# A transformer block on one core: the first token tile projected from centred rows, the last tile cut at column 336, and a new hand-written order

## Chip, cores, metric

The kernel runs on one core of one Trainium2 chip. The metric is the device time of one execution in microseconds (us); less is better. A core has TensorE (PE, with its weight loads shown as PEld), VectorE (DVE), ScalarE (ACT), GpSimd (POOL) and SyncE (SP). SP, ACT and POOL issue DMAs.

## What is computed

```
x = A_x                                   # 1 x 2048 x 448, bf16
xn = (x - mean) / sqrt(var + 1e-5)        # per row
q, k, v = xn @ wqkv                       # 16 heads of 28
attn: row s sees rows s, s-2, ..., s-14;  softmax(q.k * 28**-0.5) . v, then @ wo
g = silu(gelu(xn @ w1 + b1) @ w2 + b2)    # 448 -> 1792 -> 448
```

The kernel returns x + attn * g: lines 696 and 700 add the input row block and store it.

## The kernel before, in words

The 2048 rows are taken as two halves, even and odd positions, so that a window of every second row becomes a window of neighbours. They are cut into 16 tiles of 128 rows, and four tiles make a chunk of 512. A tile is normalised on DVE (L330, L334, L364, L369; the root is on ACT, L342, its reciprocal on DVE, L345), turned so that features lie on partitions (tiles 0 to 3 by PE, L379, with a copy out of PSUM at L229 or L231; the others by a DMA transpose, L277), and kept in xnT.

PE then does five kinds of product. Queries and keys (L455) and values (L478) have 448 columns, the first feed-forward product (L513) has 512. These three are split into pairs of 64-row halves: job a uses the upper half of the array's rows while job b uses the lower one, then they change places behind a hop over POOL or SP (L412 to L426). The second feed-forward product (L547, 14 matmuls a tile), and the output projection (L682, 4 a tile) use all 128 rows. Attention is in nine blocks; a block is 64 small matmuls of scores (L596, 32 rows by 64 columns of the array, four PSUM banks) and 64 of values (L628, 64 by 32, two banks). Between them ACT takes the exponential (L606) and POOL or DVE multiplies with a mask (L612). Behind the values a string of four DVE operations, twice a block, divides by the sum: transpose L638, reciprocal L642, transpose back L647, multiply into oT L652, which also gives the bank back. The last tile's two products are cut into two parts of 224 columns (L526 to L529). A tile ends with DVE's product of attention and gate (L688, L690), the sum with x (L696) and a DMA from SP (L700). All products share eight PSUM banks, p_b, taken in order of release.

The first two tiles take another path, first_batch (L428): the three 128-row blocks of the q, k and v weights (w_in, kt 0 to 2) are used with all 128 rows as they land, three matmuls for each of the two tiles and each block; the last 64 rows (w_in3) follow.

Each of the 942 tasks names an engine, what it needs, and the buffers that it takes and gives. Which engine it runs on and where it stands is not decided by a scheduler: the string ORDER (L17) lists every task by number with a letter for its engine (P for PE, V DVE, A ACT, G POOL, S SP, D the landing of a DMA), and emit (L95) writes the instructions in just that order. So each engine's queue is the subsequence of its letter.

At the start SP issues x of tile 0, block 0 of w_in, block 2, x of tiles 2 and 3, block 1, the two parts of w_in3, then w1. ACT issues x of tile 1. POOL makes the identity, clears b1r, loads b1 into it as rows (b1r, L308) and makes the masks (L728 to L735). PE turns b1r into a column (L769) behind the first batch. Until data is there PE multiplies zeros (L244, 17 times).

Of the kernel before, what the change touches and what calls it, by code (L numbers as in the profile page):

```python
# [10 lines left out]
ALU = mybir.AluOpType  # L11
# [6 lines left out]
D0 V1 G21 S38 A40 V19 V20 P2 V26 S42 V27 G54 D39 V28 G55 V29 V30 P3 V31 V32 S48 V33 D41 V34 G35 V22 V23 G36 P4 V24  # L18
G37 V25 D43 S44 P5 A57 S46 P6 G104 S50 P7 D49 V64 P8 S52 P9 V65 S80 G106 V68 A66 P10 D45 S82 V67 P11 P12 V110 P13
S84 P14 P15 D47 V111 P112 V69 S86 P113 G108 A70 P16 V114 P17 S90 P18 V71 A115 D116 P136 V117 D51 S92 V118 P119 D53  # L20
P120 S94 V72 P140 A121 D56 D81 A122 D123 P137 V73 V76 A74 P138 V75 V124 P139 V125 V77 D83 V105 P126 A78 A58 P127 D85
V107 P141 D87 V79 V128 D129 P142 V130 V131 P153 V109 A143 D91 V144 A148 P132 G154 P133 V149 S145 P155 A134 D135 V147
P194 A156 P312 D93 V157 G172 D95 A152 V98 G174 P317 D173 S158 D146 G313 V99 G176 V88 P314 G318 G178 V89 P319 V195
V100 G182 A315 S150 P160 G180 V101 D159 V96 A316 G103 P167 V97 A320 P322 A321 G161 G168 V204 G102 D151 P162 V205
V208 S206 V209 P169 A163 V164 G323 P324 A170 V171 S210 D207 P327 G184 A325 V200 V201 G186 V196 P332 A326 S202 D211
V197 G328 G188 P329 G333 G190 S198 P334 D203 G192 A330 P231 G250 A331 S165 D199 G284 P238 A335 G232 G256 P233 A336
G239 D183 S276 P240 D185 S278 V235 A234 D187 P219 S280 D189 D191 P212 G220 D193 S236 P221 D166 G213 P214 A222 V223
S282 P337 A215 V216 S224 D237 P342 G338 P339 G343 A241 V242 P344 A340 D277 S217 P532 A341 P537 D279 A345 G533 A346
P534 G538 D285 P539 D175 A535 V300 D177 P542 A536 D179 V301 V294 S243 D181 P547 A540 G543 D218 V295 V298 A541 P544
V299 G548 V309 P549 A545 V310 V303 P552 D244 A546 V304 V307 P557 A550 G553 V308 V305 A551 P554 D281 G558 V306 V296  # L30
G311 P559 A555 V297 P562 A556 P226 A560 V435 G563 D283 G302 V436 P564 V431 A561 S437 V432 V427 P245 A565 V428 V423
G227 S433 P228 V424 A566 A59 G246 D438 P247 V230 A229 P695 S429 A248 V249 D434 G252 P517 G286 S425 G288 D287 V359
P518 D430 G290 V360 A696 G292 A698 S361 V697 G254 D289 V347 P713 A700 D291 P512 G258 V519 D293 A702 D251 G260 V699
D362 A520 V701 G262 P513 A714 V521 A716 D253 V703 D255 A718 V715 G717 P527 D257 V514 A720 D259 V719 D261 A515 V721
D263 P572 V516 D225 V348 V351 S349 P573 V352 V355 V356 D426 S353 P522 V574 D350 A575 S357 P704 P731 V576 D354 P523
G264 A732 V705 G266 A734 V706 D265 V707 G268 A736 P528 D267 V524 D358 G270 A738 V708 G272 A525 P363 G274 D269 V529
D271 P370 V709 A530 D273 G364 G733 D275 P365 V531 S371 P372 V710 G735 A366 V367 P382 A373 V374 S368 P389 G383 V711
G737 P384 V712 S390 S375 D369 P391 V739 A385 V386 P857 A392 V393 S387 P722 P749 D376 V858 P577 G401 A750 V859 S394
V723 G405 A752 G751 A754 P578 V724 D388 V725 S860 A756 V726 G753 P567 V579 D395 V727 A580 G755 P740 P767 V728 V729
P568 G757 A768 V730 D861 A770 D402 V526 A772 D406 P867 G769 V569 A774 P458 V868 A570 P465 V869 G459 V581 S870 P460  # L40
G466 V741 G771 D871 P467 A461 V462 P453 A468 V469 S463 P472 G454 V742 G773 V743 P455 S473 S470 D464 V744 P474 G775
A456 V457 P439 A475 V476 P446 G440 D471 V745 P441 G447 V746 V747 P448 A442 V443 P872 A449 V450 S444 P862 V873 P582
V863 S451 D445 V874 V864 P758 P785 V748 S875 P583 S865 A786 V759 D452 G477 A788 G787 V760 V761 A790 P877 V762 A792
A60 G789 P377 D866 V584 D876 P587 V763 A585 S378 G791 V764 P379 V765 S588 P589 V766 A380 G793 P592 A381 V571 V878
P597 G411 S593 V879 G413 D412 P594 V586 A590 S598 G415 S880 D414 P599 G419 A591 D881 P396 D416 G403 A595 D420 G407
P602 D404 S397 A596 G409 D408 P398 A600 D410 G603 P607 A601 V399 P604 A400 G417 S608 P609 G421 D418 A605 G478 P612
D422 A606 G480 D479 P617 A610 D481 G613 G482 A611 G484 P614 D483 S618 G486 D485 P619 A615 G488 D487 P776 A616 P794
D489 G490 V777 P627 A620 G492 V778 D491 V779 A621 A61 G494 D493 P632 V780 G496 D495 V781 G498 D497 V782 P892 G500
D499 V783 G502 D501 P628 V784 G504 D503 V893 G506 D505 V894 P803 G508 D507 V629 P633 S895 A804 G510 D509 V795 A630
D896 G805 D511 V796 A806 P622 V634 A808 G807 V631 A635 P821 V797 A810 P623 G809 V798 A822 A824 V636 P637 G811 A826  # L50
V624 A828 V799 G823 A625 P812 P839 V800 V626 P638 A840 G825 V813 A842 V814 A844 P897 V815 G827 A846 A62 V639 P882
V898 A640 G829 P642 V883 P647 V899 G643 G841 V816 S900 P644 V884 S648 D901 V641 G843 P649 S885 A645 V817 P652 D886
A646 G845 V818 V819 P887 A650 S653 V820 A651 G847 P654 V888 P657 A655 V889 V801 S890 P662 A656 G658 V802 D891 P659
G663 P664 A660 P907 A661 P912 A665 V908 A666 P830 V909 P848 V913 S910 P667 V914 D911 V831 P672 S915 G668 V832 D916
V833 P669 G673 V834 P674 A670 V835 P677 A671 V836 V837 A675 P681 V838 A676 A63 V849 P678 V850 V851 V852 P917 V679
P682 V853 A680 P922 V918 P902 V683 V919 A684 P685 V903 S920 V904 D921 P686 S905 V923 D906 V924 P927 V687 S925 P689
V854 A688 D926 V855 P690 V856 P692 A691 P693 V928 V929 P932 A694 P937 S930 V933 D931 V934 S935 V938 D936 V939 S940
D941
# [61 lines left out]
def kernel(  # L120
# [19 lines left out]
    KT = 4  # L140
# [45 lines left out]
    xnT = sb("xnT", [P, KT, S])  # L186
    qkT = sb("qkT", [P, 2, G, S])
# [39 lines left out]
    def copy(e, o, i):  # L227
        if e == "ACT":
            nc.scalar.copy(o, i)  # L229
        else:  # L230
            nc.vector.tensor_copy(o, i)  # L231
# [10 lines left out]
    for i in range(17):  # L242
        def fn(k, n=512 if i < 9 else P):
            nc.tensor.matmul(buf(p_b, k)[:, :n], warm[:, :P], warm[:, :n], start=True, stop=True)  # L244
        t_warm = plan.add("PE", fn, [t_warm], take=(p_b,))
        t_warm.give = ((p_b, t_warm, 0),)
# [49 lines left out]
    def load_w(kt):  # L296
        t_w.append([dma("SP", w_in[:, kt, :], A_wqkv[kt * P:(kt + 1) * P, :])])
# [64 lines left out]
    def norm(t):  # L362
# [11 lines left out]
        halves, apart = [], t < 2  # L374
# [7 lines left out]
        n = 2 if t < 2 else 4  # L382
        copied = []
        for k0 in range(0, KT, n):
            def f4(k, k0=k0, b=halves[k0 // 2 if apart else 0]):
                copy(k.on, xnT[:, k0:k0 + n, t * P:(t + 1) * P], half_bank(buf(p_b, b))[:, k0:k0 + n, :])
            b = halves[k0 // 2 if apart else 0]
            copied.append(plan.add(("DVE", "ACT"), f4, [halves[(k0 + n - 1) // 2]], give=((p_b, b, 0),)))
        t_xT01[t], t_xT[t] = copied[0], plan.add("DMA", None, copied)
# [38 lines left out]
    def first_batch(tiles, tiles0=0):  # L428

        f = []  # L430
        for kt in range(3):
            for i, js in enumerate(tiles):
                def f1(k, kt=kt, i=i, js=js):
                    for q, j in enumerate(js):
                        j.part(buf(p_b, f[i] if kt else k, q), kt, 2, kt == 0, False)
                f.append(plan.add("PE", f1, ([t_xT01[tiles0 + i]] if kt < 2 else js[0].deps[:1]) + t_w[kt] + f[i:i + 1] * (kt > 0) + f[:1] * (i > 0), take=() if kt else (p_b,) * len(js) ))
# [12 lines left out]
    def qk_rows(t, which):  # L449
        cs = slice(t * P, (t + 1) * P)  # L450

        def part(ps, kt, half, start, stop):
            r = half_rows(half)
            w = w_in[r, kt, which * D:(which + 1) * D] if kt < 3 else w_in3[r, 0, :]
            return nc.tensor.matmul(ps[:, :D], xnT[r, kt, cs], w, start=start, stop=stop)  # L455

        def evac(a, own, i):
            b = qk_tok[t % len(qk_tok)]

            def fn(k):  # L460
                copy(k.on, b[:, which, :, :DH], buf(p_b, own, i)[:, :D].rearrange("p (h c) -> p h c", h=H))
            t_row[t].append(plan.add(("ACT", "DVE"), fn, [a, t_qz[t % len(qk_tok)], t_qk.get(t - len(qk_tok))], give=((p_b, own, i),)))
# [3 lines left out]
        return _Job(D, part, [t_xT[t]] + t_w[0] + t_w[1] + t_w[2], evac, (), t_w[3])  # L466
# [5 lines left out]
    def vproj(t):  # L472
        k0 = t * P

        def part(ps, kt, half, start, stop):
            r = half_rows(half)
            w = w_in[r, kt, 2 * D:] if kt < 3 else w_in3[r, 1, :]
            return nc.tensor.matmul(ps[:, :D], xnT[r, kt, k0:k0 + P], w, start=start, stop=stop)  # L478

        def evac(a, own, i):  # L480
            def fn(k):
                copy(k.on, v_tok[t][:, :, :DH], buf(p_b, own, i)[:, :D].rearrange("p (h c) -> p h c", h=H))
# [352 lines left out]
```

## Time and profile before

| what | value |
|---|---|
| time, median of 3 runs (lowest, highest) | 156.43 us (156.08, 156.59) |
| the profiled execution's own time | 157.63 us |
| its span, first to last instruction | 155.8 us |
| mean granted TensorE clock | 0.999 |
| busy: PE, DVE, ACT, POOL | 149.6, 110.9, 85.5, 74.2 us |
| chain that ended last: PE's share | 89% |
| first product of data at (L379), first of L513 at | 5.54, 14.17 us |
| start of the last group of products (L682) | 151.06 us |
| last output DMA issued, landed | 153.05 us, 1.5 us later |

The span is the time between first and last instruction of the profiled execution; its own time has 1.83 us beside it, and the median of the runs is 1.20 us below it. So differences are worked out in the span and then taken off the median.

### The profile page before, as it was taken

Reading aid. Unit: us, or ns where it says so; the run is one execution under the profiler, and the core shown is the slowest. Engines: PE = TensorE matmul, PEld = TensorE weight load, DVE = VectorE, ACT = ScalarE, POOL = GpSimd, SP = SyncE. Lnnn points to the kernel's source line nnn. Section 1 sums busy time; section 2 is a strip of 40 time slices with the busy share of each in tenths; the row PEclk is TensorE's granted clock in tenths of the full one; section 3 lists DMA queues with packets and bytes.
Section 4 is the critical chain, followed back from the end, with each engine's and each line's share of the span. In section 5 each row is a group of like instructions: output and inputs, shape, how many; then the busy total and the mean of one; then the engine's idle time right before and its main releaser. Section 6 shows DMA issues by size and latency. Waiting matters only on the chain.

```text
span 155.8 us, 5305 instructions
## 1 busy us (share of the span) xinstructions
PE 149.6 (96%) x2204; PEld 77.3 (50%) x2204; DVE 110.9 (71%) x254; ACT 85.5 (55%) x156; POOL 74.2 (48%) x123
## 2 busy tenths in 40 slices
PE   6899999999999999999999999999999999999990
PEld 2444444444455556554654544446556434545590
DVE  4679571387166768997799898107989996997672
ACT  3438657277888615425634196778186677192130
POOL 7852867000347808639543078389799690000000
PEclk9999999999999999999999999999999999999999
DMA  5999996999936433079219730323300010200211
GB/s 144 323 300 285 122 212 151 213 343 263 196 67 131 127 67 89 21 154 130 57 36 124 112 98 22 89 58 86 91 30 4 17 49 29 61 6 0 74 39 34
DMA packets 33575, 17.36 MB, mean 111 GB/s; under 512 B 25331, under 2 KB 32387, under 8 KB 33552
## 3 DMA queue, kind: packets, MB, share of 16 engines
q1 hardware_dynamic: 31472, 14.03, 42.8%
q0 software_dynamic: 1936, 2.88, 7.3%
q8 instruction: 17, 0.28, 0.8%
q10 hardware_dynamic: 144, 0.11, 0.3%
q14 instruction: 6, 0.05, 0.1%
HBM read 7.06 MB, written 1.84 MB: 57 GB/s over the span
## 4 chain that ended last, share of the span: by engine, by line
PE 89%; DMA 4%; DVE 2%; ACT 1%; SPq 1%; issue 0%; DVEq 0%
PE bank L547 28%; PE bank L513 27%; PE bank L455 12%; PE bank L682 8%; PE bank L478 6%; DMA x_sb<-in_A_x_dram 4%; PE bank L596 4%; PE bank L628 4%; ACT L317 1%; SPq L264 1%; DVE st L330 1%; DVE sg L688 1%; DVE xn L364 0%; ACT qk_tok L229 0%; PE bank L379 0%
## 5 line engine op out<-in xcount | busy, mean ns | idle before, releaser
L547 PE MATMUL bank<-w,h 128*128 128x448 bf16 (+1 forms) x238 | 45.2, 342 | 0.0
L513 PE MATMUL bank<-xnT,w 64*128 64x512 bf16 x392 | 44.3, 376 | 0.0
L517 ACT ACTIVATE h<-bank,b 128x512 bf16<-128x512 f32 x56 | 34.1, 687 | 15.2 <-PE bank L513 15.1
L271 POOL DMA_DIRECT2D v<-v_tok x52 | 27.5, 536 | 21.1 <-PE bank L628 8.0
L612 POOL TENSOR_TENSOR E<-E,m_gen 128x456 bf16<-128x456 bf16 x24 | 26.5, 1132 | 11.2 <-ACT E L606 8.2
L547 PEld LDWEIGHTS <-h 128*128 128x128 bf16 x238 | 22.3, 98 | 18.1 <-issue 0.4
L513 PEld LDWEIGHTS <-w 64*128 64x128 bf16 x392 | 18.8, 94 | 22.6 <-issue 0.7
L455 PE MATMUL bank<-w_in,xnT 64*128 64x448 bf16 (+1 forms) x212 | 23.7, 350 | 1.0 <-DMA w_in<-in_A_wqkv_dram 0.9
L606 ACT ACTIVATE E<-bank 128x456 bf16<-128x456 f32 (+1 forms) x36 | 17.0, 555 | 12.8 <-PE bank L596 12.8
L455 PEld LDWEIGHTS <-xnT 64*128 64x128 bf16 (+1 forms) x212 | 10.4, 94 | 11.9 <-issue 2.3
L638 DVE STREAM_TRANSPOSE dt<-bank 128x480 f32<-128x480 f32 (+1 forms) x18 | 12.1, 671 | 5.7 <-PE bank L628 5.7
L231 DVE CAST qk_tok<-bank 128x448 bf16<-128x448 f32 x16 | 9.4, 614 | 6.9 <-PE bank L455 6.3
L229 ACT CAST qk_tok<-bank 128x448 bf16<-128x448 f32 x16 | 8.4, 531 | 10.6 <-PE bank L455 9.1
L682 PE MATMUL bank<-wo,oT 128*128 128x448 bf16 (+1 forms) x68 | 14.1, 342 | 0.0
L562 DVE TENSOR_TENSOR y<-bank,b 128x448 f32<-128x448 f32 x15 | 9.3, 621 | 6.0 <-PE bank L547 6.0
L478 PE MATMUL bank<-w_in,xnT 64*128 64x448 bf16 (+1 forms) x106 | 13.2, 349 | 0.0
L647 DVE STREAM_TRANSPOSE dt<-rd 128x480 f32<-128x480 f32 (+1 forms) x18 | 12.1, 673 | 0.5
L330 DVE BATCH_NORM_STATS2 st<-x_sb 128x6 f32<-128x448 bf16 x16 | 9.7, 604 | 3.3 <-DMA x_sb<-in_A_x_dram 3.3
L574 ACT ACTIVATE t<-y 128x448 f32<-128x448 f32 x12 | 6.9, 573 | 8.9 <-DVE y L562 8.9
L652 DVE TENSOR_TENSOR oT<-bank,dt 128x456 bf16<-128x456 f32 (+1 forms) x18 | 11.3, 630 | 0.5
L364 DVE TENSOR_SCALAR xn<-x_sb,mv,rstd 128x448 bf16<-128x448 bf16 x16 | 6.4, 397 | 6.1 <-POOL rstd L352 6.0
L682 PEld LDWEIGHTS <-oT 128*128 128x128 bf16 x68 | 6.3, 98 | 6.3 <-issue 0.8
(63 smaller groups left out, 129.5 us busy)
## 6 DMA issues: line engine op xcount, KB each, us to landing
out_dram<-o SPq DMA_DIRECT2D x15, 112.0 KB, 1.7
w<-in_B_w_dram SPq DMA_DIRECT2D x2, 784.0 KB, 7.5
w<-in_B_w_dram SPq DMA_DIRECT2D x2, 672.0 KB, 7.9
x_sb<-in_A_x_dram SPq DMA_DIRECT2D x3, 448.0 KB, 6.7
v<-v_tok POOLq DMA_DIRECT2D x20, 64.0 KB, 3.0
w_in<-in_A_wqkv_dram SPq DMA_DIRECT2D x3, 336.0 KB, 6.0
w<-in_B_w_dram SPq DMA_DIRECT2D x4, 112.0 KB, 7.4
wo<-in_A_wo_dram POOLq DMA_DIRECT2D x4, 98.0 KB, 4.2
```

Source lines behind the costliest of these rows:

```text
L271: nc.gpsimd.dma_start(dst(k), src())
L455: return nc.tensor.matmul(ps[:, :D], xnT[r, kt, cs], w, start=start, stop=stop)
L478: return nc.tensor.matmul(ps[:, :D], xnT[r, kt, k0:k0 + P], w, start=start, stop=stop)
L513: return nc.tensor.matmul(ps[:], w1[r, kt, ms], xnT[r, kt, cs], start=start, stop=stop)
L517: nc.scalar.activation(buf(p_h, own, i)[:], buf(p_b, own, i)[:], ACT.Gelu_apprx_tanh, bias=b1[:, mt:mt + 1])
L547: nc.tensor.matmul(ps[:, :n], buf(*h_at[(c, mt)])[:, j * P:(j + 1) * P], w2[:, mt, cs], start=(mt == 0 and not biased), stop=(mt == NMT - 1))
L606: nc.scalar.activation(buf(p_E, k)[:, :n], buf(p_b, a, hl)[:, :n], ACT.Exp, scale=SCALE)
L612: (nc.gpsimd if k.on == "POOL" else nc.vector).tensor_tensor(out=E[:, :n], in0=E[:, :n], in1=m[:, :n], op=ALU.mult)
L638: nc.vector.transpose(buf(p_dt, k)[:, :32 * m], buf(p_b, po, i)[:, :32 * m])
L647: nc.vector.transpose(buf(p_dt, d)[:, :32 * m].rearrange("p (b c) -> p b c", c=32), buf(p_rd, r)[:, :m].unsqueeze(2).to_broadcast((P, m, 32)))
L652: nc.vector.tensor_tensor(out=oT[:, :, q0:q0 + 2 * nq], in0=buf(p_b, po, i)[:, :n].rearrange("p (l q) -> p l q", l=4), in1=buf(p_dt, d)[:, ...
L682: nc.tensor.matmul(ps[:, :n], oT[:, kt, t * P:(t + 1) * P], wo[:, kt, cs], start=(kt == 0), stop=(kt == KT - 1))
```

## The change

Seven things change. (1) A new task centre subtracts the mean of tile 0 alone; the centred rows are turned by four transposes of their own into xcT, and q, k and v of tile 0 are multiplied from there. Their copies out of PSUM multiply by rstd, one number per row. Tile 0 is still normalised and turned into xnT as well, for the feed-forward product, now in the way of tiles 2 and 3. (2) Block 0 of w_in is issued by ACT instead of SP. (3) There are 13 products of zeros instead of 17. (4) The last tile is cut into 336 and 112 columns. (5) ORDER is new from end to end, with 944 tasks. (6) In it, some tasks run on other engines: ACT copies 32 q, k and v results instead of 25; DVE does 14 mask products instead of 8, and POOL 22 instead of 28; POOL does 7 of the 17 final sums, before none. (7) The start is in another order: SP issues x of tile 0, block 2, x of tiles 2 and 3, block 1, w_in3, w1; ACT issues x of tile 1, loads its table for the root, takes one root, and then issues block 0; POOL clears b1r and makes the identity, then one mask (one memset and six selects) and a row of zeros, and issues b1's load behind these; PE turns b1r between the first two groups of the first batch.

```diff
-    for i in range(17):
-        def fn(k, n=512 if i < 9 else P):
+    for n in (512,) * 8 + (P,) * 5:
+        def idle(k, n=n):
...
-        t_w.append([dma("SP", w_in[:, kt, :], A_wqkv[kt * P:(kt + 1) * P, :])])
+        t_w.append([dma("SP" if kt else "ACT", w_in[:, kt, :], A_wqkv[kt * P:(kt + 1) * P, :])])
...
+    def centre():
+        def f1(k):
+            nc.vector.tensor_scalar(buf(p_xn, k)[:, :D], x_sb[:, 0, :], mv[:, 0, 0:1], None, op0=ALU.subtract)
+        a = plan.add("DVE", f1, [t_st[0]], take=(p_xn,))
+        def f2(_):
+            nc.vector.tensor_copy(buf(p_xn, a)[:, D:], buf(p_xn, a)[:, KF:D])
+        twice = plan.add("DVE", f2, [a])
+        turn(0, a, twice, xcT[:], True, t_c01, t_c)
...
-            return nc.tensor.matmul(ps[:, :D], xnT[r, kt, cs], w, start=start, stop=stop)
+            x = xnT[r, kt, cs] if t else xcT[r, kt, :]
+            return nc.tensor.matmul(ps[:, :D], x, w, start=start, stop=stop)
...
-                copy(k.on, b[:, which, :, :DH], buf(p_b, own, i)[:, :D].rearrange("p (h c) -> p h c", h=H))
+                copy(k.on, b[:, which, :, :DH], buf(p_b, own, i)[:, :D].rearrange("p (h c) -> p h c", h=H), None if t else rstd[:, :1])
...
-        n = D // 2 if t == NT - 1 else D
-        return [(slice(c0, c0 + n), n, c0 + n == D) for c0 in range(0, D, n)]
+        edges = (0, 336, D) if t == NT - 1 else (0, D)
+        return [(slice(c0, c1), c1 - c0, c1 == D) for c0, c1 in zip(edges, edges[1:])]
```

ORDER, from PE's letters (the numbers of tasks differ between the kernels): the products between the first feed-forward product and the end are in groups of one shape, and the new order has them in other groups, with each block of values directly behind a block of scores in six of nine cases.

More of the change, by code (lines that the diff above doesn't have):

```diff
@@ L186 @@
     xnT = sb("xnT", [P, KT, S])
+    xcT = sb("xcT", [P, KT, P])
     qkT = sb("qkT", [P, 2, G, S])
@@ L225, in buf, with copy @@
         return pool.bufs[owner.slots[pool][i]]
-    def copy(e, o, i):
+    def copy(e, o, i, by=None):
         if e == "ACT":
-            nc.scalar.copy(o, i)
+            if by is None:
+                nc.scalar.copy(o, i)
+            else:
+                nc.scalar.activation(o, i, ACT.Copy, scale=by)
+        elif by is None:
+            nc.vector.tensor_copy(o, i)
         else:
-            nc.vector.tensor_copy(o, i)
+            nc.vector.tensor_scalar(o, i, by, None, op0=ALU.mult)
     def memset(eng, ap, v):
@@ L373, in norm, with turn @@
             return
-        halves, apart = [], t < 2
+        turn(t, a, twice, xnT[:, :, t * P:(t + 1) * P], t == 1, t_xT01, t_xT)
+    def turn(t, a, twice, dst, apart, first, whole):
+        halves = []
         for i in range(2):
@@ L380, in norm, with f4 @@
             halves.append(plan.add("PE", f3, [twice if i else a, t_ident] + halves, take=() if i and not apart else (p_b,), give=((p_xn, a, 0),) if i else ()))
-        n = 2 if t < 2 else 4
+        n = 2 if apart else 4
         copied = []
         for k0 in range(0, KT, n):
-            def f4(k, k0=k0, b=halves[k0 // 2 if apart else 0]):
-                copy(k.on, xnT[:, k0:k0 + n, t * P:(t + 1) * P], half_bank(buf(p_b, b))[:, k0:k0 + n, :])
             b = halves[k0 // 2 if apart else 0]
+            def f4(k, k0=k0, b=b):
+                copy(k.on, dst[:, k0:k0 + n, :], half_bank(buf(p_b, b))[:, k0:k0 + n, :])
             copied.append(plan.add(("DVE", "ACT"), f4, [halves[(k0 + n - 1) // 2]], give=((p_b, b, 0),)))
-        t_xT01[t], t_xT[t] = copied[0], plan.add("DMA", None, copied)
+        first[t], whole[t] = copied[0], plan.add("DMA", None, copied)
+    t_c01, t_c = {}, {}
+    def centre():
[6 more added lines that the diff above has]
+        turn(0, a, twice, xcT[:], True, t_c01, t_c)
     def half_rows(half):
@@ L426, in pair, with first_batch @@
         return u
-    def first_batch(tiles, tiles0=0):
+    def first_batch(tiles):
         f = []
@@ L460, in fn @@
             def fn(k):
-                copy(k.on, b[:, which, :, :DH], buf(p_b, own, i)[:, :D].rearrange("p (h c) -> p h c", h=H))
-            t_row[t].append(plan.add(("ACT", "DVE"), fn, [a, t_qz[t % len(qk_tok)], t_qk.get(t - len(qk_tok))], give=((p_b, own, i),)))
+                copy(k.on, b[:, which, :, :DH], buf(p_b, own, i)[:, :D].rearrange("p (h c) -> p h c", h=H), None if t else rstd[:, :1])
+            t_row[t].append(plan.add(("ACT", "DVE"), fn, [a, t_qz[t % len(qk_tok)], t_qk.get(t - len(qk_tok)), None if t else t_rs[0]], give=((p_b, own, i),)))
             if len(t_row[t]) == 2:
@@ L477, in part @@
             w = w_in[r, kt, 2 * D:] if kt < 3 else w_in3[r, 1, :]
-            return nc.tensor.matmul(ps[:, :D], xnT[r, kt, k0:k0 + P], w, start=start, stop=stop)
+            x = xnT[r, kt, k0:k0 + P] if t else xcT[r, kt, :]
+            return nc.tensor.matmul(ps[:, :D], x, w, start=start, stop=stop)
         def evac(a, own, i):
             def fn(k):
-                copy(k.on, v_tok[t][:, :, :DH], buf(p_b, own, i)[:, :D].rearrange("p (h c) -> p h c", h=H))
-            t_vt[t] = plan.add(("ACT", "DVE"), fn, [a] + t_vw + v_used[t], give=((p_b, own, i),))
-        return _Job(D, part, [t_xT[t]] + t_w[0] + t_w[1] + t_w[2], evac, (), t_w[3])
+                copy(k.on, v_tok[t][:, :, :DH], buf(p_b, own, i)[:, :D].rearrange("p (h c) -> p h c", h=H), None if t else rstd[:, :1])
+            t_vt[t] = plan.add(("ACT", "DVE"), fn, [a, None if t else t_rs[0]] + t_vw + v_used[t], give=((p_b, own, i),))
+        return _Job(D, part, [t_xT[t] if t else t_c[0]] + t_w[0] + t_w[1] + t_w[2], evac, (), t_w[3])
     def values(b):
@@ L752, in project @@
             if not c and not i:
-                first_batch([js[n] + [vs[n]] for n in range(2)], t)
+                first_batch([js[n] + [vs[n]] for n in range(2)])
             else:
```

90 lines of the change are left out of this document (46 added, 44 removed).

## Prediction

> **What bounds the kernel.** I read the page first, then the chain in order of time.
>
> ```profile
> span 155.8 us, 5305 instructions
> PE 149.6 (96%) x2204; PEld 77.3 (50%) x2204; DVE 110.9 (71%) x254; ACT 85.5 (55%) x156; POOL 74.2 (48%) x123
> ```
>
> ```profile
> 62.45 5.40 PE bank L455 x56
> 67.86 0.86 PE bank L682 x4
> 68.72 0.61 PE bank L628 x64
> ...
> 147.59 0.76 PE bank L682 x4
> ```
>
> From 14 us on the chain is PE without a gap. Four products of L682 take 0.76 us beside products of the same shape, 0.86 where the shape changes behind them: a change costs 0.10. Starts in the timeline give the price of one product: 0.189 us at 448 columns with 128 rows, 0.0958 at 224, 0.0946 at 448 in pairs of 64 rows, 0.108 at 512 in pairs; 64 scores take 0.64, 64 values 0.61. All of PE's work but the zeros, so priced, is 143.6 us, and its last product is over at 151.8 (151.06 + 8 x 0.0958). So 8.2 us are lost to waits. The timeline says where:
>
> ```profile
> 6.26 0.19 POOL L728 MEMSET m<- 128x114 bf16 x1
> ...
> 7.79 0.54 PE L455 MATMUL bank<-w_in,xnT 128*128 128x448 bf16 x2 [0.63 <-DMA w_in<-in_A_wqkv_dram]
> ...
> 8.30 0.20 POOL L728 MEMSET m<- 128x112 bf16 x1
> ...
> 14.17 3.20 PE L513 MATMUL bank<-xnT,w 64*128 64x512 bf16 x28
> ```
>
> At 14.17 PE has done 6.75 us of priced work, so 7.4 are lost before it and 0.8 behind it. The start is bound by loads, the rest by PE. (The two POOL rows are used below: one mask takes 8.30 - 6.26 = 2.04 us.)
>
> **Fewer changes of shape.** I counted neighbours in both orders. Groups of 128 rows or of 64-row pairs are left for another shape 26 times before, 17 times after: -9 x 0.10 = -0.90. Four more transposes at 0.056 (four of L379 within 0.22 us): +0.22. Together **-0.68**. New is scores directly before values, six times; nearest are values before scores (last value to first score 0.126) and scores before 448 columns (0.140). I take nothing; the upper end is six changes, +0.6.
>
> **The last tile.** 15 + 4 products at 336 and at 112 columns cost as much as twice that at 224, if the price goes by columns: 0.049 at 112. But each needs a weight load:
>
> ```profile
> 5.48 0.27 PEld L379 LDWEIGHTS <-xn 128*128 128x128 bf16 x4
> ```
>
> Each of these loads lasts 0.097, yet four start within 0.17: 0.056 apart. So a product of 112 columns costs between 0.049 and, if loads stood in line, 0.098; I take 0.056, the row nearest in size: 19 x 0.007 = **+0.13** (up to +0.9). [...] The transposes above go at 56 ns.
>
> Behind the products:
>
> ```profile
> 151.06 0.93 PE L682 MATMUL bank<-wo,oT 128*128 128x224 bf16 x8
> ...
> 151.71 0.39 DVE L688 TENSOR_TENSOR sg<-bank,w_in 128x224 bf16<-128x224 f32 x1 [0.96 <-ACT w_in L569]
> 152.14 0.28 DVE L696 TENSOR_TENSOR o<-x_sb,sg 128x224 bf16<-128x224 bf16 x1
> 152.33 0.39 DVE L688 TENSOR_TENSOR sg<-bank,w_in 128x224 bf16<-128x224 f32 x1
> 152.75 0.28 DVE L696 TENSOR_TENSOR o<-x_sb,sg 128x224 bf16<-128x224 bf16 x1
> ```
>
> The second half waits for DVE to finish the first; its DMA goes out at 153.05, 1.22 behind the last product. After: the first part's four products of L682 come 1.06 us ahead of the last part's end, and its DVE work (0.50 + 0.33, by columns between the rows of 448 and 224) fits in. The last part then costs 0.2 from product to DVE (as 147.43 to 147.63), 0.27 + 0.03 + 0.20 for the two operations at 112 columns, 0.03 to the issue, and 0.05 as its gate on ACT is ready that much late: 0.78. **-0.45**. The DMA lands in 1.5 for 112 KB or 56 KB alike.
>
> **The start.** Centring takes root and reciprocal (0.29 + 0.17) out of the way to the first product, but the new order puts the second tile's statistics (0.60) ahead of the first's aggregate, so xcT is there at about 6.0, where the first product began at 6.20. And two loads are later.
>
> b1's rows: POOL now makes a mask first. 0.79 + 0.75 (clear, identity) + 2.04 + 0.2 (zeros) puts the issue at 3.8 or 3.9, before 1.82. From the views of the two tiles:
>
> ```profile
> L264 POOL DMA_DIRECT2D b1r<-in_B_b_dram x1: 694/694/694, 1.8 to 1.8; - x1
> ...
> DMA to landing us min/median/max: 4.8/4.8/4.8
> ```
>
> ```profile
> L264 SPq DMA_DIRECT2D w_in<-in_A_wqkv_dram x1: 438/438/438, 1.2 to 1.2; - x1
> DMA to landing us min/median/max: 3.3/3.3/3.3
> ```
>
> The DMA engines are as busy at 4 to 9 us as at 2 to 7 (98% to 104%), so b1 lands at 8.7; bounds 5.6 (1.7, POOL's copies of v on idle engines) to 9.3 (5.4, its copy issued at 14.15). Before, its product stood at 14.01 and waited for nothing; now it stands behind the first group of the first batch, and everything on PE is queued behind it. Done by then: 8 transposes and one group of three, 1.0. Still to do up to the second half of tile 2's pair: 5 x 0.57 (five groups) + 0.45 (tiles 0 and 2 turned) + 0.06 + 0.57 (w_in3) + 0.76 and 0.57 (tile 2's pair) + 0.22 (tile 3 turned) + 3 x 0.10 = 5.8, to 14.5, with 6.8 done: 7.7 lost instead of 7.4. **+0.3.** Behind b1, w_in's other blocks are on time: block 1, needed at 10.6, landed at 9.3 before.
>
> Block 0 is issued by ACT behind x (0.79), table (1.21 to 2.49) and a root, at 2.7, before at 1.24 and first in line. Bounds: 3.3 to landing as before, 6.0; 6.6, as the block issued at 2.68 had it, 9.3. Under 8 it hides behind b1. I take 7, nearer the low end: x of tile 1 on ACT's queue landed no later than x of tile 0 on SP's (2.5 and 2.7). [...]
>
> **Waits behind the start.** Less DVE work (-7 copies of 0.62, -7 sums of 0.39, +6 masks of 0.39) and more on ACT (+7 x 0.53 of 85.5) are off the path. But cover is thinner. I summed engine rows between a bank's use and its next taker: before, three spots behind 15 us have under 0.2 us to spare, after, about a dozen. Before, 0.8 was lost there; I add half of it, **+0.4** (0 to 1.0).
>
> **Sum.** 0.3 - 0.68 + 0.13 - 0.45 + 0.4 = -0.3: span 155.5, the profiled execution's time 157.3, the median 156.43 - 0.3 = **156.1**.
>
> **Rivals.**
> - *The start is faster.* b1 lands as on idle engines, at 5.6, and block 1 at 9.3 is the gate: from there 5 groups less three, the rest of the list above, 3.8 to 13.1, 6.3 lost: -1.1 instead of +0.3: **154.7**. For it: b1 is 3.5 KB. Against: it took 4.8 with the engines full.
> - *Block 0 late (slower).* It lands at 9.3: 6.3 of work remain to the same point, 15.6: +1.4 for the start, **157.2**. It makes the kernel slower by more than 0.5 from a landing of 8.9 on. For it: 336 KB issued late; against: the queue of its own.
> - *DVE's strings.* Scores take four of eight banks. After the fourth block of values the next scores but one come behind 5.4 us of pairs, and DVE has in between two strings (2 x 2.24), a copy, two masks, y and g, less overlaps: 5.3. Masks and g are not steady:
>
> ```profile
> L578 DVE SCALAR_TENSOR_TENSOR g<-t,y x8: 611/620/1214, 50.8 to 96.2; 128x448 bf16<-128x448 f32 x8
> L578 DVE SCALAR_TENSOR_TENSOR w_in<-t,y x4: 1066/1228/1466, 114.2 to 124.9; 128x448 bf16<-128x448 f32 x4
> ```
>
>  The long ones stand beside POOL's mask products. One long one opens the wait; two or three such spots give +1.0 instead of +0.4 and more at worst: **157.0**.
> - *The clock.* The page's row of granted clock is all 9. Between the first group and b1 PE would do nothing for some 1.5 us. At the start the products of 512 zeros took 0.427 against 0.216 later, for 3.8 us; that again costs 1.9: **158.0**. [...]
>
> **Chances.** Forecast 0.60 (155.4 to 156.9, by its own bounds), faster start 0.12, block 0 late 0.10, strings 0.12, clock 0.06. A run of this kernel can tell 0.3%, 0.47 us. Faster: 0.36 of the forecast's (0.22) and the fast start, 0.34. Slower: the three slow rivals and a little, 0.28. Within: 0.38. The range takes the nearer part of the fast start and all but the clock and the worst of the late block: 155.0 to 157.3.
>
> **What would show it.** b1's DMA issued at 3.8 and landed at 8.7, with PE waiting for it ahead of its product; the first L513 product with 9 fewer changes before the end; the last DMA 0.8 behind the last product; PE's priced work 143.1. A b1 that lands before 8, or a first product of block 0 behind 8.1, breaks the start's term; waits over 0.5 at scores or pairs break the fourth.

## The result, and the profile after

| what | before | after |
|---|---|---|
| median (lowest, highest) of 4 runs each | 156.34 us (156.08, 156.59) | 162.61 us (161.12, 164.17) |
| ratio, 95% interval | | 1.034 (1.029 to 1.040) |
| profiled execution's own time, span | 157.63, 155.8 us | 163.66, 161.9 us |
| first product of L513, after L537 | 14.17 us | 17.71 us |
| end of the last product | 151.83 us | 158.67 us |
| last output DMA issued | 153.05 us | 159.52 us |

The kernel became slower by 3.4%; 156.1 had been forecast. The profiled execution is one of two out of five in which TensorE's clock fell in the middle (mean 0.989); the three in which it did not took 161.1 to 162.4 us.

Line numbers are now those of the kernel after. The page still shows TensorE busy:

```profile
span 161.9 us, 5290 instructions
...
PE 153.7 (95%) x2204; PEld 82.7 (51%) x2204; DVE 107.9 (67%) x247; ACT 88.2 (54%) x165; POOL 73.9 (46%) x124
...
PEclk9999999999999999996999999999999999999999
...
PE 67%; DVE 16%; ACT 7%; DMA 4%; issue 2%; POOL 1%; DVEq 0%; ACTq 0%; POOLq 0%
```

The chain is what tells: PE had nearly all of it from 14 us on, now a third belongs to others. The timeline of the start (start, length, engine, line) shows the first of two places:

```profile
4.46 1.58 POOL L242 MEMSET wo<- 128x1792 bf16 x1
...
4.70 1.48 DVE L405 TENSOR_SCALAR xn<-x_sb,mv 128x448 bf16<-128x448 bf16 x1
...
6.23 0.61 PE L388 MATMUL bank<-ident,xn 128*128 128x128 bf16 x4 [0.96 <-DVE xn L405]
...
9.55 0.29 PE L795 MATMUL bank<-ident,b1r 128*128 128x128 bf16 x1 [0.95 <-DMA b1r<-in_B_b_dram]
9.63 0.95 PE L478 MATMUL bank<-w_in,xnT 128*128 128x448 bf16 x2
...
13.14 0.54 PE L478 MATMUL bank<-w_in,xnT 128*128 128x448 bf16 x2
...
17.71 2.28 PE L537 MATMUL bank<-xnT,w 64*128 64x512 bf16 x16
```

Three things are to be seen. Centring takes 1.48 us, as long as POOL's clearing of wo beside it; the normalising of the same tile took 0.40 before. PE waits for b1's rows. And two products last 0.95 us at 9.63 but 0.54 at 13.14: from 6.23 to 12.7 they start 0.373 apart instead of 0.189. The array goes at half speed, and the row PEclk says 9 all the while; only the durations tell it. (Below, the array comes up when it goes over to full speed, and falls when it goes back.)

The second place is at 72 us. First rows of DVE and POOL from 56 to 62 us, then those of PE at the place:

```profile
55.91 1.25 DVE L636 TENSOR_TENSOR E<-E,m_gen 128x456 bf16<-128x456 bf16 x1
...
59.19 1.08 POOL L636 TENSOR_TENSOR E<-E,m_gen 128x456 bf16<-128x456 bf16 x1
59.29 1.54 DVE L602 SCALAR_TENSOR_TENSOR g<-t,y 128x448 bf16<-128x448 f32 x1
...
60.75 1.23 DVE L370 TENSOR_SCALAR xn<-x_sb,mv,rstd 128x448 bf16<-128x448 bf16 x1
60.78 1.06 POOL L636 TENSOR_TENSOR E<-E,m_gen 128x456 bf16<-128x456 bf16 x1
```

```profile
71.86 0.21 PE L620 MATMUL bank<-qkT 32*64 32x57 bf16 x2
...
72.94 0.21 PE L620 MATMUL bank<-qkT 32*64 32x57 bf16 x2 [0.87 <-DVE qk_tok L235]
...
74.02 0.69 PE L620 MATMUL bank<-qkT 32*64 32x57 bf16 x58 [0.33 <-DVE oT L676]
...
75.51 1.65 PE L706 MATMUL bank<-wo,oT 128*128 128x448 bf16 x4
...
78.65 0.92 PE L706 MATMUL bank<-wo,oT 128*128 128x448 bf16 x4
```

DVE's mask product, g and xn take 1.25, 1.54 and 1.23 where they alone take 0.38, 0.62 and 0.40. DVE is late from there on, and the scores that begin at 71.86 get their four banks one by one until 74.02: 2.14 us lost. Behind that the clock falls (the 6 in PEclk): four products take 1.65, a little later 0.92.

Priced as in the prediction, span against span:

| where | us |
|---|---|
| start: time lost ahead of the first L513/L537 product, 7.93 before, 10.49 after | +2.56 |
| second pair of L537, at 18.9: its bank waits for ACT's copy of k, which stands behind ACT's second table load | +0.37 |
| scores at 71.86 (2.14), pairs ahead of them (0.51), L537 at 127.72 (0.53); before, waits at scores 0.45 | +2.73 |
| clock at half speed behind the scores (0.69 + 0.38), in this execution | +1.07 |
| values directly behind scores, six times (0.06 to 0.26) 0.82; before, values behind values 0.28 | +0.54 |
| seven fewer changes of shape behind the start (two more are in its own line) | -0.70 |
| products: four more transposes | +0.22 |
| last DMA issue behind the last product: 1.22 before, 0.85 after | -0.37 |

The sum is +6.4, and the last DMA goes out 6.5 later; the spans differ by 6.1, as 0.4 less passes behind that issue.

The start is a figure of two single executions. The edits of e4 and e8, below, leave the starts of after and of before as they are, and yet their first L538 and L513 products stand at 15.97 and 13.46, not 17.71 and 14.17: by these two the start lost 8.75 and 7.22, so +1.53.

### The profile page after: what moved, and what is told of

It reads as the page before. It is cut to its first block, busy times and chain, and to the rows that moved or that the text cites. A ratio compares the mean times of both kernels' runs of the same rounds, so it can differ in the third digit from the quotient of the medians.

```text
span 161.9 us, 5290 instructions
## 1 busy us (share of the span) xinstructions
PE 153.7 (95%) x2204; PEld 82.7 (51%) x2204; DVE 107.9 (67%) x247; ACT 88.2 (54%) x165; POOL 73.9 (46%) x124
## 4 chain that ended last, share of the span: by engine, by line
PE 67%; DVE 16%; ACT 7%; DMA 4%; issue 2%; POOL 1%; DVEq 0%; ACTq 0%; POOLq 0%
PE bank L537 24%; PE bank L571 15%; PE bank L478 9%; PE bank L706 8%; PE bank L502 5%; DMA b1r<-in_B_b_dram 4%; PE bank L652 3%; DVE dt L662 2%; DVE oT L676 2%; ACT h L541 2%; DVE y L586 2%; DVE E L636 2%; DVE g L602 2%; DVE dt L671 2%; PE bank L620 2%
## 5 line engine op out<-in xcount | busy, mean ns | idle before, releaser
L537 PE MATMUL bank<-xnT,w 64*128 64x512 bf16 x392 | 45.7, 376 | 0.3 <-DVE oT L676 0.2
L571 PE MATMUL bank<-w,h 128*128 128x448 bf16 (+2 forms) x238 | 45.8, 344 | 0.0
L277 POOL DMA_DIRECT2D v<-v_tok x52 | 27.9, 541 | 30.1 <-PE bank L388 10.8
L541 ACT ACTIVATE h<-bank,b 128x512 bf16<-128x512 f32 x56 | 34.9, 691 | 12.0 <-PE bank L537 11.9
L537 PEld LDWEIGHTS <-w 64*128 64x128 bf16 x392 | 21.7, 94 | 20.7 <-issue 1.5
L636 POOL TENSOR_TENSOR E<-E,m_gen 128x456 bf16<-128x456 bf16 x18 | 19.2, 1072 | 17.9 <-ACT E L630 11.8
L630 ACT ACTIVATE E<-bank 128x456 bf16<-128x456 f32 (+1 forms) x36 | 17.7, 555 | 14.1 <-PE bank L620 11.0
L720 POOL TENSOR_TENSOR o<-x_sb,sg 128x448 bf16<-128x448 bf16 x7 | 7.5, 1077 | 19.6 <-DVE sg L714 16.6
L706 PE MATMUL bank<-wo,oT 128*128 128x448 bf16 (+2 forms) x68 | 15.0, 355 | 0.0
L231 ACT CAST qk_tok<-bank 128x448 bf16<-128x448 f32 x21 | 10.4, 536 | 6.2 <-PE bank L478 5.0
L502 PE MATMUL bank<-w_in,xnT 64*128 64x448 bf16 (+1 forms) x102 | 13.0, 352 | 0.0
L235 DVE CAST v_tok<-bank 128x448 bf16<-128x448 f32 x6 | 3.6, 611 | 9.8 <-PE bank L502 9.8
```

The costliest lines, as they stand in the source:

```text
L277: nc.gpsimd.dma_start(dst(k), src())
L502: return nc.tensor.matmul(ps[:, :D], x, w, start=start, stop=stop)
L537: return nc.tensor.matmul(ps[:], w1[r, kt, ms], xnT[r, kt, cs], start=start, stop=stop)
L541: nc.scalar.activation(buf(p_h, own, i)[:], buf(p_b, own, i)[:], ACT.Gelu_apprx_tanh, bias=b1[:, mt:mt + 1])
L571: nc.tensor.matmul(ps[:, :n], buf(*h_at[(c, mt)])[:, j * P:(j + 1) * P], w2[:, mt, cs], start=(mt == 0 and not biased), stop=(mt == NMT - 1))
L630: nc.scalar.activation(buf(p_E, k)[:, :n], buf(p_b, a, hl)[:, :n], ACT.Exp, scale=SCALE)
```

## Experiments

Each was timed beside the kernel before, and every time and ratio is against that: 156.98 us for e1 to e4, 156.55 for e5 to e8, 156.69 for e9 to e12. Where the edit is in ORDER, the diff shows POOL's letters of the start: G50 clears b1r, G51 loads b1, G17 makes the identity, G102 the first mask, G31 and G32 the row of zeros, G33 clears wo. In the experiments' own kernels lines are one higher than in the kernel they come from (L406 is after's L405).

**e1: 17 products of zeros.**

```diff
-        def idle(k, n=n):
-            nc.tensor.matmul(buf(p_b, k)[:, :n], warm[:, :P], warm[:, :n], start=True, stop=True)
+        def idle(k, n=n, more=(512, P, P, P) if n == P and len(plan.tasks) == 11 else ()):
+            for c in (n,) + more:
+                nc.tensor.matmul(buf(p_b, k)[:, :c], warm[:, :P], warm[:, :c], start=True, stop=True)
```

> The kernel after with 17 products of zeros as before (9 of 512 columns and 8 of 128), the four added ones at the end of the first run of zeros. Theory A, half speed: in the kernel after every product from 6.23 to 12.7 us goes at half speed (0.373 against 0.189), because the zeros stop at 5.06, before the clock has come up (before, it came up at 5.4, 4.2 us into an unbroken run). With zeros up to about 5.8 the clock comes up at 5.4; the six groups behind b1's arrival then cost 1.6 us less: about 1.6 off the kernel after, 160 us. Theory B, late data: the idle time until 6.23 and from 8.4 to 9.55 takes the clock down again whatever the zeros do, or products at half speed hide behind the loads: no change, 161.5 us.

Median 163.26 us (161.04 to 166.07), ratio 1.033 (1.024 to 1.041): no gain. In its profile the array was at full speed from 4.0 us on, before the first of the added zeros (4.43). It then stood 2.2 us in front of b1 (landed 9.81, first L538 product 18.09), went at full speed for five more products and fell to half at 10.8. So in this profile the added zeros had nothing to do, and the wait for b1 took the array down again. What they do in an execution in which it comes up later, no profile shows; the times show no gain.

**e2: b1's load first.**

```diff
-G50 G17 G102 G31 G51 G32 G33 G156
+G50 G51 G17 G102 G31 G32 G33 G156
```

> The kernel after with b1's load issued on POOL right behind the clearing of b1r, ahead of identity, mask and row of zeros, as before; all else stays. Theory A, b1 is the gate: it lands at about 6.6 instead of 9.5, the 1.15 us that TensorE waited for it ahead of its turn go, and the first feed-forward product stands about 1.2 earlier than at 17.7; products remain at half speed, as the zeros still stop at 5.06. About 160.4 us. Theory B, the next load binds: blocks 1 and 2 of w_in land at 9.0 and 5.6, and the feed-forward weights at 15.7 to 16.1; TensorE would stand in front of these instead: 161.3 us or more.

162.02 us (160.97 to 162.4), ratio 1.032 (1.027 to 1.036). b1 landed at 5.86 and was no gate; the first L538 product stood at 15.97. But the clearing of wo came 0.7 later and met the next operation instead:

```profile
4.49 0.32 DVE L406 TENSOR_SCALAR xn<-x_sb,mv 128x448 bf16<-128x448 bf16 x1
...
5.01 1.76 DVE L410 COPY xn<-xn 128x64 bf16<-128x64 bf16 x1
...
5.16 1.58 POOL L243 MEMSET wo<- 128x1792 bf16 x1
```

Centring is fast without the clearing, and a copy of 64 columns takes 1.76 us with it (0.16 in e3, without it). So neither theory was whole: the time won at b1 went to the clearing and to half speed (until 10.8).

**e3: b1's load first, and wo cleared behind the identity.**

```diff
-G50 G17 G102 G31 G51 G32 G33 G156
+G50 G51 G17 G33 G102 G31 G32 G156
```

> As the run with b1 first, and POOL's clearing of wo (1.58 us) moved to directly behind the identity, so that it is over before tile 0 is centred. Theory A: the centring took 1.48 us instead of 0.40 because it ran beside that clearing (4.46 to 6.04); without it xcT's first transposes come at about 5.2, right behind the zeros, TensorE runs unbroken and comes up to full speed at about 5.4, and of the 2.9 us that the start lost most is back: 158.6 us. Theory B: the centring is slow for a reason of its own (a first use, the operation's form): it stays at 1.4 and the time is that of the run with b1 first, 160.4 us.

160.43 us (160.12 to 161.5), ratio 1.024 (1.019 to 1.028); the first L538 product at 13.52, 6.30 us lost ahead of it (before: 7.93).

```profile
2.58 1.59 POOL L243 MEMSET wo<- 128x1792 bf16 x1
...
4.66 0.38 DVE L406 TENSOR_SCALAR xn<-x_sb,mv 128x448 bf16<-128x448 bf16 x1
```

Theory A holds for the start: 4.2 us earlier than after. The whole is only some 1 to 2 us faster, because the scores still lost 2.10 us and the clock fell behind them for 1.48.

**e9: wo cleared early, b1's load behind the mask.**

```diff
-G50 G17 G102 G31 G51 G32 G33 G156
+G50 G17 G33 G102 G31 G51 G32 G156
```

> The kernel after with only POOL's clearing of wo moved ahead of the mask, so that b1's load goes out 1.6 us later still, at about 5.3. It shares the fast centring with the run that has b1 and wo first (160.4 us, first feed-forward product at 13.5). Theory A, b1 gates the start once its turn stands in the first batch: b1 lands at 10 to 11, TensorE waits for it from 6.8 on, 3 to 4 us, and goes at half speed for a while behind so long a wait: first feed-forward product at 17.5 to 18.5, 164 us. Theory B, other loads gate it anyway: 13.5 to 14, 160.4 us.

166.51 us (165.48 to 169.14), ratio 1.062 (1.057 to 1.068), more than either theory said. b1 was issued at 5.24 and landed at 11.64:

```profile
6.12 0.95 PE L479 MATMUL bank<-w_in,xcT 128*128 128x448 bf16 x2
...
11.68 0.29 PE L796 MATMUL bank<-ident,b1r 128*128 128x128 bf16 x1 [4.18 <-DMA b1r<-in_B_b_dram]
11.77 0.95 PE L479 MATMUL bank<-w_in,xnT 128*128 128x448 bf16 x2
...
16.30 0.58 PE L503 MATMUL bank<-w_in,xnT 128*128 128x448 bf16 x1
...
17.66 0.35 PE L503 MATMUL bank<-w_in,xcT 128*128 128x448 bf16 x1
```

With a fast centring as in e3 (0.32 us), the first L538 product stands 7.5 us later (21.05). b1 is a gate: 4.3 us of waiting, and then half speed from 11.7 to 17.4, 5.7 us. Here the array had come up, at 7.2, and fell behind the wait.

**e10: the kernel before with wo cleared behind the first mask.**

```diff
-G21 G54 G55 G35 G36 G37 G104 G106 G108
+G21 G54 G55 G35 G36 G104 G37 G106 G108
```

> The kernel before with POOL's clearing of wo moved behind the first mask, so that it runs from about 4.7 to 6.3, beside the normalising of tile 0 (4.98 and 5.41). Theory A, shared access: normalising or the copy behind it takes 1.0 to 1.4 us longer and the first product of data stands that much later; half to all of it is seen at the first feed-forward product (14.17 before): 157 to 158 us. Theory B, only the new centring is slow beside it: 156.5 us, no change.

156.95 us (156.92 to 158.01), ratio 1.003 (1.001 to 1.005).

```profile
4.59 1.59 POOL L237 MEMSET wo<- 128x1792 bf16 x1
...
5.09 1.22 DVE L365 TENSOR_SCALAR xn<-x_sb,mv,rstd 128x448 bf16<-128x448 bf16 x1
```

The old normalising, 0.40 before, is held up in the same way, so it isn't the new operation. Its price is small here: first product of data at 7.04, but the first product of L513 at 13.67, no later than before: the array was at full speed (0.55 us for the two products at 7.04) and b1 is no gate there. What PE lost at 7 us it would probably have lost to loads: in the profile of before it waited for w_in at 7.79 and 9.31 (0.63 and 0.23), here not at all.

**e12: the kernel before with 13 products of zeros.**

```diff
-        def fn(k, n=512 if i < 9 else P):
-            nc.tensor.matmul(buf(p_b, k)[:, :n], warm[:, :P], warm[:, :n], start=True, stop=True)
+        def fn(k, n=512 if i < 9 else P, leave=i in (8, 13, 15, 16)):
+            if not leave:
+                nc.tensor.matmul(buf(p_b, k)[:, :n], warm[:, :P], warm[:, :n], start=True, stop=True)
```

> The kernel before with 13 products of zeros: one of 512 and one of 128 columns fewer ahead of the first data, two of 128 fewer behind. Theory A, the clock: the zeros end at about 5.0 instead of 5.54, and where the clock has not come up by then, products of data start at half speed (0.373 each) until some 3 us of unbroken work have gone by: first feed-forward product 1 to 1.5 later, 157.5 us. Theory B, the gap up to the first data is only 0.5 us, the clock comes up in it or at its end as before: 156.6 us.

156.85 us (155.88 to 157.63), ratio 1.000 (0.997 to 1.003). Theory B: the array came up at 4.4 and stayed up. Fewer zeros alone cost nothing that ten executions show.

**e4: three mask products from POOL to DVE.**

```diff
-G721 G719 G739
+V721 V719 V739
```

> The kernel after with three mask products (those that POOL runs at 59.2, 60.8 and 62.3 us) given to DVE. Theory A, shared access: three of DVE's operations beside them took 1.54, 1.23 and 1.06 us instead of 0.62, 0.40 and 0.18; without them DVE is 2.6 ahead and has 3 x 0.38 more to do, so the scores at 71.9 us wait 0.7 to 1.5 us less than the 2.15 that they did: about 160.5 us. Theory B, DVE has too much to do there whoever runs beside it: it gets 1.1 us more, the wait is longer, 162.5 us.

160.22 us (159.48 to 161.44), ratio 1.024 (1.018 to 1.030). In the same stretch as above, and at the scores:

```profile
56.98 0.62 DVE L603 SCALAR_TENSOR_TENSOR g<-t,y 128x448 bf16<-128x448 f32 x1
...
57.52 0.39 DVE L371 TENSOR_SCALAR xn<-x_sb,mv,rstd 128x448 bf16<-128x448 bf16 x1
...
69.77 0.48 PE L621 MATMUL bank<-qkT 32*64 32x57 bf16 x6
...
70.57 0.65 PE L621 MATMUL bank<-qkT 32*64 32x57 bf16 x58 [0.33 <-DVE oT L677]
```

g and xn are back at their own times. DVE has three products more to do and is earlier: 0.75 lost at the scores instead of 2.14, nothing at the pairs, and the clock stays up. This is theory A. (The start came out 1.74 us earlier than in after with nothing changed there; e5 against e3, whose starts are edited alike, is free of that.) A second such place became plain:

```profile
119.48 1.06 POOL L637 TENSOR_TENSOR E<-E,m_gen 128x456 bf16<-128x456 bf16 x1
...
120.11 2.27 DVE L721 TENSOR_TENSOR o<-x_sb,sg 128x448 bf16<-128x448 bf16 x1
...
121.06 1.06 POOL L637 TENSOR_TENSOR E<-E,m_gen 128x456 bf16<-128x456 bf16 x1
...
125.00 9.87 PE L538 MATMUL bank<-xnT,w 64*128 64x512 bf16 x89 [0.61 <-DVE oT L677]
```

A sum that takes 0.39 alone takes 2.27 beside two masks, the string behind it is late, and PE waits for its multiply into oT.

**e5: e3 and e4 together.**

```diff
-G50 G17 G102 G31 G51 G32 G33 G156
+G50 G51 G17 G33 G102 G31 G32 G156
-G721 G719 G739
+V721 V719 V739
```

> The kernel after with both mends: b1's load and the clearing of wo ahead of the first mask on POOL, and three mask products from POOL to DVE. Theory A, two separate losses that both come from DVE held up beside POOL: they add up. The start gets to the first feed-forward product by 13.5 to 14, the scores wait 0.75, no fall of the clock behind them: e3's 160.4 less 2.1 to 3.5, so 157 to 158.3. Theory B, time won at the start is lost again in the middle, as the same loads and queues bind there: no better than the mend of the masks alone, 160.2.

158.36 us (157.32 to 159.89), ratio 1.010 (1.006 to 1.014). The two add up: first L538 product at 13.64, 0.87 lost at the scores (2.10 in e3, which differs by the three masks alone), no fall of the clock, 1.09 still lost at the values of 119 us. What DVE has ahead of them this time is g, beside two masks of POOL:

```profile
116.57 2.50 DVE L603 SCALAR_TENSOR_TENSOR g<-t,y 128x448 bf16<-128x448 f32 x1
```

**e6: e5, two more masks on DVE, two copies of q and k on ACT.**

```diff
-G813 G829 V376 V388
+V813 V829 A376 A388
```

> As the run with both mends, and two more mask products from POOL to DVE (those beside which DVE's sum x + sg took 2.27 us at 120 us), and two copies of q and k at about 70 us from DVE to ACT. Theory A, shared access: the wait of 0.97 at the first feed-forward products of about 124 us goes, the one at the scores falls from 0.75 to about 0.2; 1.3 less than the run with both mends: 155.7 to 157. Theory B, too much on DVE: the two masks add 0.76 to its strings at 124 us and the wait there stays at 0.9 or grows; ACT's copies come later than DVE's: no better than with both mends.

155.38 us (155.18 to 156.81), ratio 0.993 (0.989 to 0.997): faster than both kernels. The second place is gone, and the scores lose 0.34 (what the masks and what the copies did for it was not taken apart):

```profile
span 154.1 us, 5289 instructions
...
PE 149.4 (97%) x2204; PEld 80.4 (52%) x2204; DVE 103.0 (67%) x250; ACT 89.2 (58%) x167; POOL 69.2 (45%) x119
```

DVE got five products more than in the kernel after (and gave two copies of 0.6 away), and is busy 4.9 us less.

**e7: e3, and all 22 masks of POOL on DVE.**

```diff
 each of the 22 letters G of a mask product in ORDER
-G
+V
```

> The kernel after with b1 and wo first and all 22 mask products of POOL on DVE. Theory A, shared access: the 22 cost DVE 8.4 us, and its operations of two SBUF inputs, its bf16 copies and its products with a number per row all go at their short times; about as fast as the run with five masks moved, 156 to 157.5, with DVE's busy time no more than 5 us above 107. Theory B, DVE's own load decides: 8 us more on it make the scores and values wait; over 160.

157.2 us (156.94 to 157.86), ratio 1.002 (0.999 to 1.006). The groups of DVE, first of after, then of e7 (line, operation, form, count, busy us, mean ns):

```profile
L602 DVE SCALAR_TENSOR_TENSOR g<-t,y 128x448 bf16<-128x448 f32 x9 | 7.4, 819 | 1.4 <-ACT t L598 1.4
...
L636 DVE TENSOR_TENSOR E<-E,m_gen 128x456 bf16<-128x456 bf16 x10 | 6.5, 653 | 0.0
```

```profile
L637 DVE TENSOR_TENSOR E<-E,m_gen 128x456 bf16<-128x456 bf16 x28 | 10.4, 381 | 0.7 <-ACT E L631 0.7
...
L603 DVE SCALAR_TENSOR_TENSOR g<-t,y 128x448 bf16<-128x448 f32 x9 | 5.9, 652 | 1.4 <-ACT t L599 1.4
```

DVE's page total is 106.9 us with 22 masks more, against 107.9. The load is not what made DVE late. It is still 1.8 us slower than e6: behind the start PE loses 2.0 us (e6: 0.74), at the values of 68 us (0.61) and at 107 and 113 us (0.60, 0.37). So theory B has a share; what waits there was not followed up.

**e8: the kernel before, last tile 336 and 112.**

```diff
-        n = D // 2 if t == NT - 1 else D
-        return [(slice(c0, c0 + n), n, c0 + n == D) for c0 in range(0, D, n)]
+        edges = (0, 336, D) if t == NT - 1 else (0, D)
+        return [(slice(c0, c1), c1 - c0, c1 == D) for c0, c1 in zip(edges, edges[1:])]
```

> The kernel before with the last tile in parts of 336 and 112 columns, nothing else. By the prediction's terms: 19 products at 112 columns cost 0.049 to 0.056 each, the last output DMA goes out 0.78 to 0.86 behind the last product where it was 1.22: 0.3 to 0.4 us less than before (0.2%). If loads of weights held the short products up (0.098 each), or the long first part came too late for DVE: 0.4 more or level.

156.77 us (156.13 to 158.45), ratio 1.001 (0.997 to 1.005): level. The 112-column products start 0.049 apart, so loads of weights hold nothing up. But in the order before, all eight products of L682 stand at the end, and DVE's four operations come behind them:

```profile
150.26 0.93 PE L682 MATMUL bank<-wo,oT 128*128 128x336 bf16 x8
...
151.10 0.51 DVE L688 TENSOR_TENSOR sg<-bank,w_in 128x336 bf16<-128x336 f32 x1 [1.15 <-PE bank L682]
151.64 0.33 DVE L696 TENSOR_TENSOR o<-x_sb,sg 128x336 bf16<-128x336 bf16 x1
151.89 0.27 DVE L688 TENSOR_TENSOR sg<-bank,w_in 128x112 bf16<-128x112 f32 x1
152.19 0.22 DVE L696 TENSOR_TENSOR o<-x_sb,sg 128x112 bf16<-128x112 bf16 x1
```

The last DMA goes out 1.41 behind the last product, before 1.22.

**e11: e6, last tile 224 and 224.**

```diff
-        edges = (0, 336, D) if t == NT - 1 else (0, D)
+        edges = (0, D // 2, D) if t == NT - 1 else (0, D)
```

> The fastest kernel so far (five masks moved, b1 and wo first, two copies on ACT; 155.4 us) with the last tile in parts of 224 and 224 again. By the traces the parts of 336 and 112 have the last output DMA 0.86 behind the last product, where the kernel before had 1.22, and products cost the same by columns: 0.3 to 0.5 us slower with 224, 155.8 us. If the order, which puts the first part's last products ahead of the second part, does the work and not the sizes: within 0.15 of 155.4.

155.71 us (155.42 to 157.23), ratio 0.997 (0.994 to 1.000); the times of e6 and e11 cannot be told apart by their intervals. The traces can: the last DMA goes out 1.00 behind the last product, 0.85 in e6. Of the 0.37 at the end, 0.22 come from the order and 0.15 from the sizes.

## Why the prediction was wrong

**The start, +0.3 forecast, +2.56 and +0.37 measured.** Two steps failed, both behind b1: "b1 lands at 8.7", and the price of a product, 0.189, taken for certain where it was a state. The forecast queues everything on PE behind b1's product. Behind that its list has 5.8 us of work, and the eight L502 products ahead of the first L537 are 0.76 more, 6.6 in all. The profiles fit one sum: the first L537 (or L538) product stands 6.5 us behind b1's, and later by half of the time that the array goes at half speed in between (by the changes of the granted clock in the trace).

| profile | b1's product | half speed behind it | sum | first L537 or L538 |
|---|---|---|---|---|
| after | 9.55 | 3.30 | 17.70 | 17.71 |
| e1 | 9.86 | 3.41 | 18.07 | 18.09 |
| e2 | 8.10 | 2.69 | 15.95 | 15.97 |
| e4 | 8.46 | 1.96 | 15.94 | 15.97 |
| e9 | 11.68 | 5.77 | 21.07 | 21.05 |

```profile
8.46 0.29 PE L796 MATMUL bank<-ident,b1r 128*128 128x128 bf16 x1
...
15.97 2.28 PE L538 MATMUL bank<-xnT,w 64*128 64x512 bf16 x16
```

(These rows are e4's.) In e3, with b1's product at 6.75 and no half speed behind it, the sum is 13.25 and the product stands at 13.52, with 0.2 of waiting at 8.7. Against a b1 at 8.7 and full speed, after lost 0.85 by a later b1 and 1.65 by half speed. Together that is about the miss of this term.

A third step was wrong too, "xcT is there at about 6.0": the first product of xcT stands at 7.09. The step counted what the change puts into DVE's queue, and of POOL's queue only what stands ahead of b1's load. The clearing of wo, which the mask pushes from 2.94 to 4.46, stood in no step, and it held up centring by 1.1 us; e2, e3 and e10 show that from three sides. But in after PE was through with all that stands ahead of b1's product by 8.4, so the late centring was hidden behind b1, as the forecast itself would have had it. It costs where b1 is early: e3's first L538 product is 2.45 ahead of e2's.

b1's issue was foreseen (3.65, forecast 3.8), and that it gates (e9). Issued at the same time in after, e1 and e4, it landed at 9.51, 9.81 and 8.42; the upper bound, 9.3, was too low for two of the three. Block 0's load was mis-sized to the other side: ACT issued it at 1.29 and not behind its table load, and it landed at 5.75. The 0.37 was not foreseen: ACT's second table load (1.28 us at 16.98) stands ahead of copies of q and k that give banks back, in after and in all of its variants.

**The clock.** It was a rival, 158.0 with a chance of 0.06. How long a pause the clock stands no run had shown; in the profile of before the waits of 0.63 and 0.23 us at 7.79 and 9.31 left it up. The profile of after shows half speed without any fall: the zeros were over at 5.06, PE stood still until 6.23, and the array came up only at 12.85, 3.3 us after b1. In e1 and e9 it had come up, and fell behind the wait for b1 (2.2 and 4.3 us). So in these profiles half speed goes with a late b1, with a late centring (3.30 us behind b1 in after) and without one (5.77 in e9); e3, with neither, has it only up to its first two products of xcT, at 5.95 (0.66 us for the two, 0.54 later). The times of e1 and e12 show nothing for the number of zeros. Whether the array of after would have come up with an early centring and b1 at 9.5 was not tried.

**Waits behind the start, +0.4 forecast, +2.73 and +1.07 of clock measured.** This term missed by the most. The place was right: the scores that come behind the 5.4 us of pairs, in the rival "DVE's strings" (157.0, chance 0.12). Its size failed twice. From the end of the values at 65.96 to the last bank at 74.02 DVE takes 8.1 us, not 5.3. The sum of DVE's rows counted one y, and there are three (+1.1); a wait of 0.4 for ACT stands in between; and the same list of operations takes some 6.6 us by the starts of their rows, so the "less overlaps" took off too much. And the step "the long ones stand beside POOL's mask products" was priced as a single one of 0.6. In fact DVE lost 0.92 at g, 0.83 at xn, 0.88 at a copy and 0.87 at a mask, all between 55 and 62 us, where the new order has five masks on POOL (55.9 to 63.4), and came late to the y's. e4 and e5 show what that is worth: three masks less on POOL, 1.4 and 1.2 less at the scores. The rest, 0.75 and 0.87, is DVE's load or what is left of the masks; that was not taken apart.

The traces show which of DVE's operations are held up beside POOL's clearing of wo or its mask products: centring, normalising, bf16 copies, masks, g and x + sg, up to 2.27 against 0.39 (x + sg, e4) and 2.50 against 0.62 (g, e5), while y, which reads a bank, takes 0.61 to 0.63 throughout, beside a mask product of POOL too (0.61 at 57.08 in after). The clearing of wo held them up as a mask product did: centring took 1.48 beside it (after) against 0.38 (e3), a copy 1.76 (e2) against 0.16 (e3), normalising 1.22 (e10) against 0.40 (before). By what they are held up no run shows.

**Changes of shape, -0.68 forecast.** Counted and priced rightly: 9 fewer at 0.09 to 0.11, and 0.22 for the transposes. The step that took nothing for scores directly before values failed: five blocks of values behind products took their 0.608 and no more, the six behind scores 0.06 to 0.26 longer, in e6 too (0.06 to 0.24). 0.82 in all, less 0.28 that two pairs of values blocks cost before; so this term is about -0.15. What delays these values was not tried.

**The last tile, -0.45 and +0.13 forecast, -0.37 and 0 measured.** The mechanism holds, the cost of small products was 0.049 and not 0.056.

So the gains were real and small, and the price lay in b1's place in POOL's queue, in half speed behind the waits, and in what DVE does beside POOL: e6, which keeps the rest of the change and mends these, lies 0.7% below the kernel before.

## What to carry to other kernels

When a step moves on POOL's queue, walk on to what it pushes, and lay every POOL operation beside DVE's rows: here centring, normalising, bf16 copies, masks, g and x + sg were held up beside POOL's clearing and mask products (g up to 2.50 us for 0.62), and y was not (0.61 to 0.63). Add up an engine's rows between a bank's use and its next taker from the order itself, each operation counted, and price the wait with what lies beside. A wait of 2 us on TensorE can cost more than 2 us: here 2.14 us at the scores were followed by 1.07 at half speed. And where two late things meet at one gate, as centring and b1 do here, mending one tells little of the other's price.

## What the runs showed of the hardware

- Half speed behind short waits. In the profiles of after, e1, e2, e3 and e9 the scores lost about 2.1 us and the clock fell behind them (1.07 us lost in after, 1.48 in e3), though it did not fall in every execution of after; in those of e4 to e7 they lost 0.26 to 0.87 and it stayed up. In after the 2.14 us have six small products in them, and four products of L706 behind them took 1.65 us, 0.92 once the clock was up again.
- The moment of coming up moves between the profiles in which the array came up on the zeros and the work behind them: 5.46 us in before, 4.0 in e1, 4.4 in e12, 7.2 in e9.
- How long the clock stays. In the trace of after the granted clock comes up at 12.85 us, is 0.50 from 74.29 to 77.70 and 1.00 again from there to the end of the span: 61.44 us up, 3.41 us down.
- The row PEclk does not show half speed at the start: all 9 in after from 6 to 13 us, with products 0.373 apart up to 12.7.
- The 3.5 KB load of b1, issued by POOL, took 4.5 us to land in e2, 4.8 in before, 5.9 in after and 6.4 in e9, while the other loads ran.
